# Slot scatters of two batches written together, and the search for the order of all instructions run again, in an attention and mixture-of-experts kernel

## The chip, the cores and the metric

The kernel runs on one core of one Trainium2 chip. The metric is the time of one execution on the device in microseconds (us). Before the change three runs gave a median of 989.69 us (986.74 to 997.49). A further execution was recorded by the profiler; it took 985.76 us, of which 983.7 us lie between its first and its last instruction (the span). All rows below come from that one execution.

The engines are called PE (matmul), PEld (its weight loads), DVE, ACT, POOL and SP. SP computes nothing here; it issues transfers.

## The reference

```python
def rmsnorm(x, g):
    return x / np.sqrt(np.mean(x * x, axis=-1, keepdims=True) + 1e-06) * g
q_n, k_n = rmsnorm(q, g_q), rmsnorm(k, g_k)      # q, k, v: (8, 12, 448, 64)
scores = 1.0 / np.sqrt(64) * np.matmul(q_n, k_n.transpose(0, 1, 3, 2))
attn = np.exp(scores - scores.max(-1, keepdims=True))
attn = attn / (attn.sum(-1, keepdims=True) + 1e-09)
x = np.matmul(attn, v).transpose(0, 2, 1, 3).reshape(3584, 768)

logits = x @ w_gate                               # 8 experts
e_idx = np.argmax(logits, axis=1)                 # one expert for each token
gate_w = softmax(logits)[range(3584), e_idx]
eom = 1.0 / (1.0 + np.exp(-(x @ w_output_gate)))
for e in range(8):
    mask = e_idx == e
    h = np.maximum(x[mask] @ w1[e], 0.0)          # 768 -> 1024
    out[mask] = gate_w[mask, None] * eom[mask, e, None] * (h @ w2[e])
```

## The kernel before, in words

**Two stages.** The first is attention with the routing of the tokens, the second the eight experts. The first stage works on pairs of heads: a batch has 6 pairs, so there are 48, numbered i = 0 to 47. Float32 values are split into an fp16 high part and an fp16 low part, and a product is made of three fp16 products.

**One pair.** `Lt` loads q and k (tile `qkt`). `sq`, `mh`, `ms`, `n`, `qg` normalise them. `hi` and `lo` split them into tile `X`, and SP transposes both parts into tile `ss` (`Th` for the high part, `Tl` for the low one; line L601). On PE, `M0` to `M3` multiply high parts alone to find the row maxima, which DVE reduces (`x0` to `x3`, tile `Z`). `NT` and `nt` turn the maxima around. `S0` to `S3` make the scores less the maximum (tile `pss`). `e`, `f` and `p` make the exponentials and their low parts (`p` is L685, on POOL or on DVE). `A0` to `A6` multiply with v into one PSUM bank, `bank_a`. `av1`, `av2` (tile `rc`) and `av` (tile `xr`) divide by the row sum on DVE; only then may `A0` of the next pair write the bank. `tr`, `th`, `lg`, `la` transpose the result and sum up the logits of the gate.

**Routing.** After the 6 pairs of a batch b, `r{b}.first` to `r{b}.val` pick each token's expert and its place (slot) in that expert's list. Four scatters `r{b}.z0` to `z3` on POOL (L925, `tab<-val,slot`) then write number and weight of 112 tokens each into a table in HBM. The experts later read the table to gather their tokens.

**What sets the order.** Nothing is ordered by hand. `Order.run` is a planner: it knows for each operation its engine, a duration, what it waits for, which buffer rings it holds, and a key. On each engine it takes, of the operations that are ready by its own reckoning, the one with the lowest key, and writes the instructions down in that order, which the chip then follows engine by engine. The keys come from the tables `ORDER` (four numbers for each operation of a pair) and `SHIFT` (one for each of the others). `SECOND` says, pair by pair, whether an operation that two engines can do goes to the first or the second of them. For a transfer the planner adds `lat`, the time until it has landed, and `xfer`, for how long it holds the one line in which the planner sees all transfers wait. Where the planner sees PE idle for long it writes dummy matmuls (L1473, `bank_a<-nil`) to keep PE active.

**The second stage** is written in a fixed order by `moe`, except for its beginning: the first expert's tokens (`ti0`, `xg0`, `xh0`, `xl0`, `xt0`; tiles `tie`, `xge`, `x16e`, `xTe`) and weights (`ld`, `wh`, `wl`; tiles `wste`, `w0he`, `w0le`) are planned among the last pairs, so that its first product (L1269 to L1271) can follow the last pair. The tokens of expert 0 are gathered as soon as the slots of batch 6 are in the table.

Of the kernel before, what the change touches and what calls it, by code (L numbers as in the profile page):

```python
# [52 lines left out]
    ("Lt", -1541.068, 1.677, 1123.974, -3.183),  # L53
    ("sq", 166.144, -220.427, 190.481, -54.246),
    ("mh", 159.818, -3.125, 104.389, 5.287),
    ("ms", 1654.033, 375.716, 0.250, 431.806),
    ("n", 551.031, -8.140, 172.786, 3247.925),
    ("qg", -0.547, -872.245, -2.714, 16.920),
    ("hi", 2613.749, 51.225, -727.417, 20.921),
    ("Th", 1224.882, -2107.533, -676.244, 4.206),  # L60
    ("lo", 111.461, 11.612, 1262.051, 1.977),
    ("Tl", 1.545, -2.870, 1456.809, 0.776),
    ("M0", -1345.132, -4.028, -113.895, -1.939),
    ("x0", 36.980, 9010.506, 1329.451, 1.959),
    ("M1", -2.241, 100.513, -909.486, 0.149),
    ("x1", 608.011, 17.341, -0.367, -618.082),
    ("M2", -5482.967, 14.685, 421.979, -0.160),
    ("x2", -40.558, 1.246, 95.915, -1.934),
    ("M3", -10.471, 10.436, 1.367, -0.606),
    ("x3", -0.247, 18.302, -113.316, 0.192),  # L70
    ("NT", 4.526, -2.542, -27.126, -365.406),
    ("nt", -423.381, -66.627, 436.237, 0.703),
    ("S0", 0.577, 0.094, 2069.489, -0.612),
    ("e0", -3.632, -247.548, 101.520, 1.675),
    ("f0", -749.332, -2.522, 1.532, -0.093),
    ("p0", 3.590, 1.506, 160.998, 6.230),
    ("S1", -0.528, -9.144, 303.627, 0.420),
    ("e1", -204.641, 1126.114, -0.554, -813.297),
    ("f1", 4.356, 13.958, -4.391, 8.716),
    ("p1", 126.230, -1037.208, 3.646, 1.070),  # L80
    ("S2", 0.890, -54.590, 1930.221, -0.702),
    ("e2", -2.506, 14.444, 324.586, -657.467),
    ("f2", 540.362, 925.892, -2165.612, 0.154),
    ("p2", -2.390, 395.783, 318.133, -413.006),
    ("S3", -0.173, -46.677, 156.691, -3.198),
    ("e3", -39.653, -12.452, -2.907, -0.161),
    ("f3", -42.192, 813.999, 1.848, 1.742),
    ("p3", -8954.383, -66.083, 437.056, 5.186),
    ("Lv", 307.167, -399.620, 2.028, 0.347),
    ("vh", -51.574, 13.836, 1122.447, 9.050),  # L90
    ("vl", 3.377, -27.833, 1857.127, -0.140),
    ("A0", 183.060, -8.172, 4581.120, 3.050),
    ("A1", 49.095, 358.907, -66.223, 484.461),
    ("A2", -23.494, 6.575, 147.243, -68.363),
    ("A3", 10.693, 870.234, 378.391, -1094.638),
    ("A4", 377.730, 1829.632, -509.308, 37.460),
    ("A5", 5.057, -1036.297, -1031.958, 3.872),
    ("A6", 111.289, 50.560, 10.150, 6.072),
    ("av1", -17.835, -40.302, -0.734, 0.797),
    ("av2", -3.174, -26.893, 0.998, -120.693),  # L100
    ("av", -32.125, 1.874, -447.062, 2.901),
    ("tr", -5.451, -22.518, -0.430, 8.606),
    ("th", -13.076, -28.146, 602.450, 40.981),
    ("lg", 56.165, -1284.148, 420.074, 480.839),
    ("la", 120.553, 469.327, -8.211, 2.397),
# [11 lines left out]
STICK = 22.539  # L117
# [17 lines left out]
    "p0": "011110 010010 111110",  # L135
    "p1": "101011 010001 100001",
    "p2": "110000 000000 101000",
    "p3": "111001 000101 001000",
    "lo": "111000 010001 000110",
    "vh": "001101 001000 000110",  # L140
    "th": "001100 000001 001001",
    "n": "011010 000100 110011",
    "qg": "111010 100101 001110",
    "nt": "001001 100110 001101",
    "ms": "111100 111011 110010",
    "sq": "010000 000000 110010",
# [7 lines left out]
    "k.cst": 169.441,  # L154
    "k.gd": 0.934,
    "k.wg": 5.408,
    "k.blank": -705.083,
    "k.xs": -6.407,
    "k.tab": 6.203,
    "k.g": -3.552,  # L160
    "k.ltri": 0.102,
    "k.flat": -5.412,
    "k.edges": -1.869,
    "s0": 841.221,
    "r": 4.116,
    "st": -228.929,
    "s": -344.165,
    "r-2": -1534.073,
    "r-1": -3.042,
    "open1": -814.841,  # L170
    "open2": -2.457,
    "ld0": 3.365,
    "wh0": -3.210,
    "wl0": 1.491,
    "ld1": -225.412,
    "wh1": -492.219,
    "wl1": -13.263,
    "ld2": -12.985,
    "ti0": -190.958,
    "xg0": -8.726,  # L180
    "xh0": -1155.543,
    "xl0": -1.884,
    "xt0": -3.974,
    "ti1": -228.290,
    "xg1": 4.112,
    "xh1": 5.976,
    "xl1": -0.744,
    "xt1": 73.295,
    "ti2": -492.239,
    "xg2": -469.933,  # L190
    "xh2": 199.918,
    "xl2": -12.676,
    "xt2": -5.019,
    "units": -12.564,
    "g1": -3.361,
    "hh": 589.316,
    "hl": -88.333,
    "g2": 104.405,
    "o0": -2.815,
    "o1": -2.734,  # L200
    "sc": -384.484,
    "k.id": -0.297,
    "k.sel0": 1061.513,
    "k.sel1": -218.223,
    "k.zero": -260.024,
    "w": 1.148,
    "z0": -492.602,
    "z1": -4.622,
    "z2": 6759.920,
# [1438 lines left out]
```

## Time and profile before

| | |
|---|---|
| median of three runs | 989.69 us (986.74 to 997.49) |
| profiled execution | 985.76 us, span 983.7 us, granted clock 0.987 |
| PE, PEld | 933.8 us busy (95%), 671.3 us (68%) |
| DVE, ACT, POOL | 619.5 us (63%), 554.1 us (56%), 426.0 us (43%) |
| first product of the experts (L1269) | at 521.0 us |

An engine's busy time is the union of its instructions' times. The time outside the span, 985.76 less 983.7, is 2.1 us. PE is busy in nearly all of the span, so other engines cost time only where PE waits for them, or where PE runs at the lower of its two clocks (the granted clock is then 0.50).

### The profile page before, as it was taken

How to read it: one execution, taken by the hardware profiler on the slowest of the kernel's cores; microseconds unless marked ns; L12 is line 12 of the kernel's file. 1: busy time of each engine (PE TensorE's matmuls, PEld its weight loads, DVE VectorE, ACT ScalarE, POOL GpSimd, SP SyncE). 2: the span in 40 equal slices, each digit the busy share in tenths (PEclk: the TensorE clock that was granted, in tenths of full speed). 3: DMA queues.
4: the chain of work that ended last, by engine and by line, in shares of the span. 5: the costliest groups of instructions: out<-in, count | busy, mean ns of one | idle time of the engine just before them, and what ended most of it. 6: DMA issues, size and time to landing. Idle time of an engine off the chain costs nothing. (4 is left out here: it accounts for less than half of the span.)

```text
span 983.7 us, 28910 instructions
## 1 busy us (share of the span) xinstructions
PE 933.8 (95%) x12551; PEld 671.3 (68%) x12551; DVE 619.5 (63%) x1043; ACT 554.1 (56%) x820; POOL 426.0 (43%) x325
## 2 busy tenths in 40 slices
PE   7898989999999999999989999999999999999997
PEld 3676667676777767777776686686776767665664
DVE  7879985897988888896565546428335263545310
ACT  6686876797887877868653435325234242525110
POOL 4476858678595988865532303112121111111101
PEclk9999998999999999999989999999999999999999
DMA  6848695686966968553655878839738386678101
GB/s 189 171 125 178 158 163 103 160 160 137 168 138 165 174 147 169 131 91 80 181 174 162 238 252 242 219 85 259 183 113 231 105 242 179 191 203 226 62 1 48
DMA packets 182542, 157.41 MB, mean 160 GB/s; under 512 B 152448, under 2 KB 160262, under 8 KB 176268
## 3 DMA queue, kind: packets, MB, share of 16 engines
q1 hardware_dynamic: 176652, 133.28, 56.8%
q0 software_dynamic: 5760, 22.25, 7.5%
q8 instruction: 100, 1.64, 0.7%
q14 instruction: 30, 0.25, 0.1%
HBM read 96.73 MB, written 22.59 MB: 121 GB/s over the span
## 5 line engine op out<-in xcount | busy, mean ns | idle before, releaser
L631 DVE TENSOR_REDUCE Z<-psM 128x2 f16<-128x896 f32 x168 | 178.4, 1084 | 35.2 <-PE psM L616 33.3
L685 POOL TENSOR_TENSOR pl<-p,ph 128x896 f16<-128x896 f32 x76 | 143.2, 1890 | 81.2 <-DVE psl L883 18.9
L717 PE MATMUL bank_a<-vf,pf 128*128 128x65 f32 (+1 forms) x896 | 150.7, 282 | 7.1 <-DVE xr L735 6.8
L1284 POOL DMA_INDIRECT out<-oe,tie x24 | 26.2, 1094 | 258.8 <-DVE oe L1306 222.3
L658 PE MATMUL pss<-ss 64*128 64x448 f16 (+1 forms) x1152 | 125.4, 354 | 6.7 <-ACT pf L670 3.3
L717 PEld LDWEIGHTS bank_a<-vf,pf 128*128 128x128 f32 (+1 forms) x896 | 111.0, 182 | 26.7 <-issue 10.1
L1269 PE MATMUL g1e<-xTe,w0he 128*128 128x384 f16 x384 | 125.2, 326 | 0.0
L1271 PE MATMUL g1e<-xTe,w0le 128*128 128x384 f16 x384 | 125.2, 326 | 0.0
L1270 PE MATMUL g1e<-xTe,w0he 128*128 128x384 f16 x384 | 125.2, 326 | 0.0
L721 PE MATMUL bank_a<-vh,pl 128*128 128x65 f16 (+1 forms) x1088 | 123.9, 196 | 0.2 <-POOL pl L685 0.2
L721 PE MATMUL bank_a<-vh,ph 128*128 128x65 f16 (+1 forms) x1088 | 123.6, 196 | 0.0
L719 PE MATMUL bank_a<-vl,ph 128*128 128x64 f16 (+1 forms) x1088 | 123.3, 194 | 0.0
L680 ACT ACTIVATE ph<-pss 128x896 f16<-128x896 f32 x112 | 102.3, 924 | 17.5 <-PE pss L664 17.4
L721 PEld LDWEIGHTS <-ph 128*128 128x128 f16 (+1 forms) x1088 | 111.1, 118 | 0.0
L721 PEld LDWEIGHTS <-pl 128*128 128x128 f16 (+1 forms) x1088 | 91.2, 101 | 0.3 <-POOL pl L685 0.3
L719 PEld LDWEIGHTS <-ph 128*128 128x128 f16 (+1 forms) x1088 | 91.3, 103 | 0.0
L1271 PEld LDWEIGHTS <-w0le 128*128 128x128 f16 x624 | 60.6, 98 | 24.8
L676 ACT ACTIVATE p<-pss 128x896 f32<-128x896 f32 x76 | 68.6, 915 | 15.7 <-PE pss L664 15.6
L1270 PEld LDWEIGHTS <-w0he 128*128 128x128 f16 x624 | 60.7, 98 | 23.9
L1269 PEld LDWEIGHTS <-w0he 128*128 128x128 f16 x624 | 60.7, 98 | 23.8
L597 POOL TENSOR_TENSOR X<-qkt,X 128x512 f16<-128x512 f32 x62 | 70.8, 1169 | 13.9 <-ACT X L593 6.2
L670 ACT ACTIVATE pf<-pss,lnv 128x896 f32<-128x896 f32 x56 | 56.4, 1010 | 31.2 <-PE pss L664 31.2
(328 smaller groups left out, 2284.6 us busy)
## 6 DMA issues: line engine op xcount, KB each, us to landing
wste<-w SPq DMA_DIRECT2D x48, 1024.0 KB, 7.0
qkt<-qkt SPq DMA_DIRECT2D x48, 448.0 KB, 4.6
vf<-v SPq DMA_DIRECT2D x48, 260.0 KB, 3.6
xs<-xr SPq DMA_DIRECT2D x16, 576.0 KB, 4.7
ss<-X SPq DMA_TRANSPOSE x96, 3.5
xs<-xr SPq DMA_DIRECT2D x16, 96.0 KB, 6.5
tab<-val,slot POOLq DMA_INDIRECT x32, 5.0
xge<-xs,tie POOLq DMA_INDIRECT x24, 4.9
```

The lines of the kernel that those rows point to most:

```text
L597: return [E.tensor_tensor(out=X[:, 1, :, :, d], in0=x, in1=X[:, 0, :, :, d], op=ALU.subtract) for x, d in sides(self.qkt.pop(i))]
L631: V.tensor_reduce(out=o, in_=m, op=ALU.max, axis=AX.X, negate=True)
L658: T.matmul(out, lhsT=side(wk, 1, h, 128 * u, n, x), rhs=side(wq, 0, h, 0, S, x), start=k == 0, stop=False)
L676: A.activation(out=t, in_=st[f"S{u}"], func=AF.Exp)
L680: A.activation(out=t, in_=st[f"S{u}"], func=AF.Exp)
L685: return (V if eng == DVE else Pl).tensor_tensor(out=t, in0=st[f"e{u}"], in1=at[f"ph{u}"], op=ALU.subtract)
L717: T.matmul(out, lhsT=st[f"pf{u}"][:, k, q], rhs=vf[:, jv, :], **go)
L719: T.matmul(out[:, 0:D], lhsT=at[f"ph{u}"][:, k, q], rhs=vl[:, jv, :], start=False, stop=False)
L721: T.matmul(out, lhsT=at[f"p{'hl'[w // 2]}{u}"][:, k, q], rhs=vh[:, jv, :], **go)
L1269: nc.tensor.matmul(o, lhsT=wh[:, sl], rhs=xT[:, 0, k, 0:n], start=k == 0, stop=False)
L1270: nc.tensor.matmul(o, lhsT=wh[:, sl], rhs=xT[:, 1, k, 0:n], start=False, stop=False)
L1271: q["mm"] = nc.tensor.matmul(o, lhsT=wl[:, sl], rhs=xT[:, 0, k, 0:n], start=False, stop=k == KD - 1)
```

## The change

Three things change; the arithmetic of the reference does not.

1. Scatters. Before, `z0` of a batch waits for its own slots and weights, and `z1`, `z2`, `z3` moreover for the division `av` of the second, third and fourth pair of the next batch (not in the last two batches). Now the four scatters of batches 0, 2 and 4 wait for slots and weights of the next batch too, and the waits for `av` are gone. So eight scatters come together, once in two batches. Batches 6 and 7 stay by themselves.
2. The planner's price of a scatter. Before, each holds the transfers for 350 ns; now the first of a batch 2,200 ns and the others 300. Its landing changes from 2,900 to 3,200 ns (first) and 3,000 (others); in the last two batches it was 5,500 for each and is that now for the first alone.
3. All keys (`ORDER`, `SHIFT`), the choice of engines (`SECOND`) and `STICK` have new numbers.

```diff
 ORDER = (
-    ("Lt", -1541.068, 1.677, 1123.974, -3.183),
+    ("Lt", -479.694, -2.008, -6.167, 6.015),
...
-STICK = 22.539
+STICK = 20.629
...
 SECOND = {
-    "p1": "101011 010001 100001",
+    "p1": "101010 010001 100100",
-    "n": "011010 000100 110011",
+    "n": "001010 000100 100100",
...
 SHIFT = {
-    "z0": -492.602,
-    "z1": -4.622,
-    "z2": 6759.920,
-    "z3": 48282.823,
+    "z0": -2.299,
+    "z1": -0.686,
+    "z2": 7651.187,
+    "z3": 60387.755,
...
         for c in range(NC):
-            add(f"z{c}", POOL, 1040, "slot val" + f" av.{NP * b + NP + c}" * (c > 0 and b < self.B - 2) + ("".join(f" r{b - 1}.z{k}" for k in range(NC)) if b else " k.tab k.blank"), lambda c=c: scatter(c), (), 5500 if b >= self.B - 2 else 2900, 350)
+            add(f"z{c}", POOL, 1040, "slot val" + f" r{b + 1}.slot r{b + 1}.val" * (b % 2 == 0 and b < self.B - 2) + ("".join(f" r{b - 1}.z{k}" for k in range(NC)) if b else " k.tab k.blank"), lambda c=c: scatter(c), (), (5500 if b >= self.B - 2 else 3200) if c == 0 else 3000, 2200 if c == 0 else 300)
```

PE gets the same products as before. Of the dummy matmuls L1473 there are 598 in place of 653; 272 in place of 306 stand ahead of `A0` of pair 0, and none of the 36 that stood before `M1` of pair 14 and before `M2` of pairs 21, 27 and 33 is left. Five `p` move from POOL to DVE, three `n` and one `qg` from DVE to POOL, seven `vh` from ACT to DVE.

**Three places in the order.** The first is POOL where batch 0 is scattered before: `pl9_2` is `p2` of pair 9, `X2` with `qkt14` is `lo` of pair 14, `slot0` are the slots of batch 0.

```order
L685 TENSOR_TENSOR pl9_2_2763<-p329_2_2720,ph9_2_2742 128x896
L925 DMA tab_87<-val_83,slot0_2513 30720x2 x2
L597 TENSOR_TENSOR X2_120<-qkt14_1707,X2_120 128x8x64 x2
L685 TENSOR_TENSOR pl10_1_2958<-p3210_1_2887,ph10_1_2903 128x896
L925 DMA tab_87<-val_83,slot0_2513 30720x2
L685 TENSOR_TENSOR pl10_2_3026<-p3210_2_2976,ph10_2_3010 128x896
```

The same place on POOL now, from `p2` of pair 9 to `p2` of pair 10:

```order
L685 TENSOR_TENSOR pl9_2_2751<-p329_2_2685,ph9_2_2711 128x896
L597 TENSOR_TENSOR X2_120<-qkt14_1672,X2_120 128x8x64 x2
L685 TENSOR_TENSOR pl10_1_2853<-p3210_1_2779,ph10_1_2795 128x896
L597 TENSOR_TENSOR X0_118<-qkt15_1757,X0_118 128x8x64 x2
L597 TENSOR_TENSOR X1_119<-qkt16_1882,X1_119 128x8x64 x2
L570 TENSOR_TENSOR sq21_3028<-sq21_3028 128x14x32
L685 TENSOR_TENSOR pl10_2_3064<-p3210_2_2964,ph10_2_3040 128x896
```

And POOL two batches on, where batches 0 and 1 are scattered now. Two scatters of batch 0 have gone out nine operations of other kinds earlier, just ahead of `lo` of pair 22; the other six are here, beside `p` of pairs 18 and 19:

```order
L580 TENSOR_TENSOR qkt28_4065<-qkt28_4065,y41_4401 128x896
L580 TENSOR_TENSOR qkt29_4204<-qkt29_4204,y41_4401 128x896
L585 TENSOR_TENSOR qkt29_4204<-qkt29_4204,g_75 128x448
L925 DMA tab_87<-val_83,slot0_2478 30720x2 x2
L685 TENSOR_TENSOR pl19_3_4649<-p3219_3_4533,ph19_3_4550 128x896
L685 TENSOR_TENSOR pl18_1_4685<-p3218_1_4631,ph18_1_4647 128x896
L925 DMA tab_87<-val_83,slot1_3852 30720x2 x4
```

All scatters of batch 0 have left the neighbourhood of pairs 9 and 10. Counted as runs of scatters with no other POOL work between them, those of batches 0 to 5 stand in 15 runs before (each of one or two) and in 10 now: 2, 2, 4 for batches 0 and 1; 4, 2, 2 for 2 and 3; 3, 1, 2, 2 for 4 and 5.

The second place is DVE where pair 3 is divided (`rc3`, `xr0`), before; `pl5_1` is `p1` of pair 5:

```order
L597 TENSOR_TENSOR X1_119<-qkt7_372,X1_119 128x8x64 x2
L585 TENSOR_TENSOR qkt9_904<-qkt9_904,g_75 128x448
L685 TENSOR_TENSOR pl5_1_1659<-pss5_1_1586,ph5_1_1619 128x896
L726 TENSOR_SCALAR rc3_1666<-bank_a_70 128x7
L729 RECIPROCAL rc3_1666<-rc3_1666 128x7
L735 TENSOR_TENSOR xr0_1075<-bank_a_70,rc3_1666 128x7x64
```

The same on DVE now:

```order
L597 TENSOR_TENSOR X1_119<-qkt7_367,X1_119 128x8x64 x2
L585 TENSOR_TENSOR qkt9_870<-qkt9_870,g_75 128x448
L726 TENSOR_SCALAR rc3_1631<-bank_a_70 128x7
L729 RECIPROCAL rc3_1631<-rc3_1631 128x7
L735 TENSOR_TENSOR xr0_1041<-bank_a_70,rc3_1631 128x7x64
```

`p1` of pair 5 no longer stands ahead of the division of pair 3; it has gone to POOL.

The third place is DVE where pair 45 is divided (`rc45`, `xr7`), before; `w0le0` is the low part of expert 0's weights, `x16e0` that of its tokens:

```order
L1166 SCALAR_TENSOR_TENSOR w0le0_10834<-wste0_0_10612,w0he0_10833 128x1024 x2
L726 TENSOR_SCALAR rc45_10979<-bank_a_70 128x7
L729 RECIPROCAL rc45_10979<-rc45_10979 128x7
L1166 SCALAR_TENSOR_TENSOR w0le0_10834<-wste0_1_10836,w0he0_10833 128x1024
L735 TENSOR_TENSOR xr7_10452<-bank_a_70,rc45_10979 128x7x64
L1237 TENSOR_TENSOR x16e0_0_11001<-xge0_10831,x16e0_0_11001 128x768
```

The same on DVE now:

```order
L1166 SCALAR_TENSOR_TENSOR w0le0_10647<-wste0_1_10619,w0he0_10646 128x1024 x2
L685 TENSOR_TENSOR pl46_2_10861<-pss46_2_10784,ph46_2_10838 128x896
L726 TENSOR_SCALAR rc45_10902<-bank_a_70 128x7
L729 RECIPROCAL rc45_10902<-rc45_10902 128x7
L735 TENSOR_TENSOR xr7_10352<-bank_a_70,rc45_10902 128x7x64
L1166 SCALAR_TENSOR_TENSOR w0le0_10647<-wste0_2_10799,w0he0_10646 128x1024
L1237 TENSOR_TENSOR x16e0_0_10947<-xge0_10694,x16e0_0_10947 128x768
```

The weight split has left the middle of the division. Between the last `A` of pair 45 and `A0` of pair 46, PE has `lg` of pair 43 and `S0` of pair 47 before, and `S0` of pair 46, `S2` of pair 47, `tr` of pair 44 and `S0` of pair 47 now.

## Rows read from the trace of the kernel before

**Rows 1.** The page: span, busy time and share of the engines.

```profile
span 983.7 us, 28910 instructions
...
PE 933.8 (95%) x12551; PEld 671.3 (68%) x12551; DVE 619.5 (63%) x1043; ACT 554.1 (56%) x820; POOL 426.0 (43%) x325
```

**Rows 2.** Windows: stretch, length, busy time by engine, granted clock (PEclk), DMA share, GB/s.

```profile
83.42:86.82 3.40, 3.40 (x49) 2.77 (x46) 2.42 (x4) 1.42 (x3) 3.40 (x4) 0.50 0.94 234
144.86:155.08 10.22, 10.21 (x84) 7.55 (x86) 4.40 (x7) 4.29 (x7) 5.20 (x4) 0.50 0.38 98
503.26:510.08 6.82, 6.82 (x83) 6.66 (x84) 2.88 (x4) 1.61 (x2) 0.00 (x0) 0.50 0.80 151
520.84:983.65 462.81, 455.63 (x3879) 305.80 (x3879) 202.34 (x274) 161.68 (x214) 75.47 (x65) 1.00 0.61 169
```

**Rows 3.** Waits of PE from 60 to 520.84 us: total, times, longest.

```profile
PE bank_a L717 <- DVE xr L735: 6.2, 6, 2.2
PE psM L616 <- DMA ss<-X: 4.4, 2, 3.9
```

**Rows 4.** Timeline of SP at 135.5 us (start, length): `Th` of pair 14.

```profile
135.50 2.59 SPq L601 DMA_TRANSPOSE ss<-X  x1
```

**Rows 5.** Timeline of POOL at 135 us: `z0` and `z1` of batch 0.

```profile
135.36 1.13 POOL L925 DMA_INDIRECT tab<-val,slot  x1 [0.17 <-DVE Z L631]
136.80 0.95 POOL L925 DMA_INDIRECT tab<-val,slot  x1 [0.30 <-issue]
```

**Rows 6.** Timeline of PE at 144.9 us: `M2` of pair 14; in brackets the idle time before.

```profile
144.87 0.56 PE L616 MATMUL psM<-ss 64*128 64x448 f16 x2 [3.89 <-DMA ss<-X]
```

**Rows 7.** Line L601, all 96 transposes of `X`.

```profile
DMA to landing us min/median/max: 3.0/3.5/6.0
```

**Rows 8.** Line L925, all 32 scatters.

```profile
DMA to landing us min/median/max: 2.3/5.0/8.0
```

**Rows 9.** Line L925 from 136.7 to 137.7 us, the scatter issued at 136.80 alone.

```profile
DMA to landing us min/median/max: 7.8/7.8/7.8
```

**Rows 10.** Line L925 from 475 to 481 us: the four scatters of batch 6.

```profile
L925 POOL DMA_INDIRECT tab<-val,slot x4: 938/942/943, 475.8 to 479.6; - x4
...
DMA to landing us min/median/max: 3.7/4.1/5.7
```

**Rows 11.** Timeline of PE at 82.9 us: `tr` of pair 2.

```profile
82.85 0.63 PE L745 MATMUL pstr<-cst,xr 128*128 128x128 f32 x4 [1.57 <-DVE xr L735]
```

**Rows 12.** Timeline of DVE at 80.7 us: `p1` of pair 5.

```profile
80.65 1.08 DVE L685 TENSOR_TENSOR pl<-pss,ph 128x896 f16<-128x896 f32 x1
```

**Rows 13.** Timeline of PE at 503.1 us: `A0` of pair 46.

```profile
503.14 0.62 PE L717 MATMUL bank_a<-vf,pf 128*128 128x65 f32 x2 [2.20 <-DVE xr L735]
```

**Rows 14.** Timeline of DVE at 500 us: within the division of pair 45.

```profile
499.88 2.67 DVE L1166 SCALAR_TENSOR_TENSOR w0le<-wste,w0he 128x1024 f16<-128x1024 f32 x1
502.47 0.61 DVE L735 TENSOR_TENSOR xr<-bank_a,rc 128x448 f32<-128x448 f32 x1
```

**Rows 15.** Timeline of PE from 118.1 us: `lg` of pair 5, and `A0` of pair 7.

```profile
118.14 0.42 PE L757 MATMUL pslg<-xT,wg 128*32 128x112 f32 x8
...
118.69 0.44 PE L717 MATMUL bank_a<-vf,pf 128*128 128x65 f32 x2
...
120.55 0.44 PE L717 MATMUL bank_a<-vf,pf 128*128 128x65 f32 x2 [1.15 <-DVE xr L735]
```

**Rows 16.** Groups of instructions: the dummy matmuls; busy, mean ns, idle before.

```profile
L1473 PE MATMUL bank_a<-nil 128*128 128x56 f16 x653 | 21.2, 191 | 1.2 <-DVE xr L735 1.2
```

**Rows 17.** Tile xTe at 514.9 us: the last transpose of expert 0's tokens.

```profile
L1247 SPq DMA_TRANSPOSE xTe<-x16e x1: 1448/1448/1448, 514.9 to 514.9; - x1
...
DMA to landing us min/median/max: 3.7/3.7/3.7
```

**Rows 18.** Timeline of PE at 521 us: the first product of the experts.

```profile
521.00 0.33 PE L1269 MATMUL g1e<-xTe,w0he 128*128 128x384 f16 x1
```

**Rows 19.** Timeline of SP at 289 us: `Th` of pair 29.

```profile
288.96 1.23 SPq L601 DMA_TRANSPOSE ss<-X  x1
```

**Rows 20.** Timeline of PE at 292.7 us: `M2` of pair 29.

```profile
292.68 0.69 PE L616 MATMUL psM<-ss 64*128 64x448 f16 x4
```

More of the change, by code (lines that the diff above doesn't have):

```diff
@@ L64 @@
[L64 to L85, printed above, removed]
@@ L97 @@
[L97 to L105, printed above, removed]
+    ("Lt", -479.694, -2.008, -6.167, 6.015),
+    ("sq", -4.752, -417.839, 3790.106, -0.585),
@@ new lines @@
+    ("S1", -1.051, -0.577, 1488.111, 0.068),
+    ("e1", -372.287, 33.550, -91.059, 40.625),
+    ("f1", 2.884, 65.836, 166.124, 2.197),
+    ("p1", 829.204, 3.407, 114.788, 9.633),
+    ("S2", -0.084, -48.663, 3455.910, -0.021),
+    ("e2", 2.989, 268.778, -472.353, -194.937),
+    ("f2", 252.451, 0.426, -116.588, -233.241),
+    ("p2", 2.914, 3.142, -1083.311, -176.328),
+    ("S3", 11.912, -14.950, -5.055, -21.970),
+    ("e3", -0.780, 1.029, -3.038, -2.847),
+    ("f3", -0.676, 566.316, -2.785, 2.314),
@@ new lines @@
+    ("p3", 2.810, 1311.103, 15.226, 4.011),
+    ("Lv", -1.085, 521.693, -389.705, 638.477),
+    ("vh", -97.421, 268.590, -48.130, 4.144),
+    ("vl", 0.494, -17.571, 5.327, -0.303),
+    ("A0", 253.322, 166.429, -411.335, -3.910),
+    ("A1", 17.766, 6623.530, -338.481, 351.146),
+    ("A2", -186.211, 0.473, -1.144, 0.611),
+    ("A3", -2.787, 317.529, 441.011, -349.866),
+    ("A4", 264.275, 1.470, -472.097, 6.182),
+    ("A5", 4.708, -397.767, 0.097, 4.513),
+    ("A6", 108.465, 29.428, 94.964, 3.438),
@@ L153 @@
 SHIFT = {
[L154 to L206, printed above, removed]
-    "z0": -492.602,
-    "z1": -4.622,
-    "z2": 6759.920,
-    "z3": 48282.823,
+    "k.cst": 0.540,
+    "k.gd": -9.009,
+    "k.wg": -4.035,
+    "k.blank": -4.137,
+    "k.xs": 3.492,
+    "k.tab": 0.586,
+    "k.g": -1.407,
+    "k.ltri": -4.270,
+    "k.flat": 220.207,
+    "k.edges": 154.898,
+    "s0": -1.990,
+    "r": 0.833,
+    "st": -251.004,
+    "s": -369.577,
+    "r-2": -3.945,
+    "r-1": -139.884,
+    "open1": 32.584,
+    "open2": -2.221,
+    "ld0": -1.147,
+    "wh0": -4.189,
+    "wl0": -0.646,
+    "ld1": -2.526,
+    "wh1": 32.217,
+    "wl1": -1.633,
+    "ld2": -350.188,
+    "ti0": -4.052,
+    "xg0": -2.771,
+    "xh0": -684.761,
+    "xl0": 1097.191,
+    "xt0": 7651.016,
+    "ti1": -979.915,
+    "xg1": -4.365,
+    "xh1": -3.812,
+    "xl1": 351.201,
+    "xt1": 2.555,
+    "ti2": 66439.632,
+    "xg2": 1.275,
+    "xh2": -3.256,
+    "xl2": 289.223,
+    "xt2": -0.998,
+    "units": -1.053,
+    "g1": -6.471,
+    "hh": 2.983,
+    "hl": 1.410,
+    "g2": 0.576,
+    "o0": 0.507,
+    "o1": -1236.661,
+    "sc": -0.991,
+    "k.id": -0.316,
+    "k.sel0": -1142.315,
+    "k.sel1": -0.918,
+    "k.zero": -2.612,
+    "w": -304.938,
+    "z0": -2.299,
+    "z1": -0.686,
+    "z2": 7651.187,
+    "z3": 60387.755,
 }
```

70 lines of the change are left out of this document (39 added, 31 removed).

## Prediction

> **What bounds the kernel now.** I began with the page: PE is busy 933.8 of 983.7 us, no other engine more than 63% [rows 1]. So time can only be won where PE waits or runs slowly. Windows by stretch then split the span. From 520.84 us on, the experts' stage, PE is busy 455.6 of 462.8 us at the full clock [rows 2]; its order is written down and the change leaves it alone, so I hold these 463 us fixed. The change must earn or lose its time in the first 521 us. PE's waits there are led by two kinds: the bank of the products with v is not yet free (6.2 us in 6 waits), and a transposed tile has not landed (4.4 us in 2, one of 3.9) [rows 3]. The third view is the windows of granted clock: 0.50 (1.2 of 2.4 GHz) for 3.4, 10.2 and 6.8 us [rows 2], each straight after one of PE's longer waits: 1.57 us [rows 11], 3.89 us [rows 6] and 2.20 us [rows 13]. PE is busy in all of them, so half their length is lost: 1.7, 5.1 and 3.4 us. A wait here costs more than its length.
>
> **The wait at batch 0's scatters.** `Th` of pair 14 was issued at 135.50 us [rows 4], 0.14 us after the first scatter and 1.3 before the second [rows 5]. PE got the tile at 144.87 [rows 6]: 9.4 us, where the median transpose takes 3.5 and the slowest one shown 6.0 [rows 7]. The second scatter landed 7.8 us after 136.80, at 144.6 [rows 9], 0.2 us before PE went on. So I put the delay on the scatters. The Trainium skill (page "DMA: Bandwidth & Descriptors", section "Queues, rings and completion order") says that the increment which reports a transfer done lands only after every earlier write of that transfer engine, across its queues. By that rule a transpose behind a scatter reports late even though its data have moved; the trace agrees in the 0.2 us above. The change takes batch 0's scatters away from pairs 9 and 10, and the next transposes there have only loads beside them. Gain: 3.9 of wait and 5.1 of half clock, **-9.0 us**.
>
> **What the scatters cost in their new places.** The same 24 scatters of batches 0 to 5 now stand in 10 runs, not 15. The trace has no run of eight or six; the nearest is batch 6's four, issued from 475.8 to 479.6 with a slowest landing of 5.7 [rows 10], so that the last is down by 485.3 at the latest, 9.5 us after the first issue. Batch 0's two were under way from 135.36 to 144.6, 9.3 us. A longer run exposes later transfers for no longer than a short one, so I price by the run. Before, 15 runs cost PE the two transfer waits, 4.4 us [rows 3], and the 5.1 of clock: 9.5, or 0.63 a run. Ten runs: **+6.3**. The bounds are 0 (no run meets a transpose that PE needs soon) and a full 9.0 for each group that does. POOL itself: one issue follows another by (479.6 - 475.8) / 3 = 1.27 us [rows 10], so a run of four holds POOL for 5.1 us, and `p2` of pair 18, queued behind batch 1's four, is up to 2.6 later than behind a run of two. Its readers are the `A`s of that pair, and PE has scores and maxima of later pairs in between; I take 0, with 2.6 for each such run as the bound.
>
> **The division of pair 3.** `tr` of pair 2 waited 1.57 us for DVE [rows 11], and `p1` of pair 5, 1.08 us from 80.65 on [rows 12], stood directly ahead of the division; it goes to POOL. So the wait falls by 1.1. Half clock followed for 3.4 us; PE's dummies, 38 of them, fill part of it, so I count half of its 1.7: **-1.9** in all, bounds 0 and -3.3.
>
> **The division of pair 45.** `A0` of pair 46 waited 2.20 us [rows 13], since a weight split of 2.67 us stood between reciprocal and division [rows 14]. It has left, and PE has four operations instead of two to do meanwhile. With the 3.4 us of clock, 5.6 could go. But what would be late next is the start of the experts: the last transpose of expert 0's tokens was issued at 514.9 and landed 3.7 later [rows 17], at 518.6, and the first product began at 521.00 [rows 18]. That chain begins with batch 6's slots and is not made shorter by PE, so I count only the **-2.4** between the two. Bounds 0 and -5.6.
>
> **Smaller ones.** `lg` of pair 5 moves from ahead of the last `A` of pair 6 to behind it, into the 1.15 us for which `A0` of pair 7 waited; it lasts from 118.14 to 118.69 [rows 15]: **-0.6**. Dummies: 55 fewer at 21.2 / 653 = 0.032 us [rows 16] is 1.8, but 34 of them stand in the first microseconds, where PE waits for data anyway; I take **-1.2**, bounds -0.7 and -1.8. `A0` of pair 20 now has only `NT` between it and the pair before, with four small DVE operations inside the division; that costs about one wait of the kind of [rows 3], 6.2 / 6 = 1.0. The similarly bare `A0` of pair 31 has got five PE operations ahead of it in exchange: 0. The five `p` that go to DVE, 5 x 1.08 [rows 12] = 5.4 us, and the seven `vh` are set against three `n` and one `qg` that leave it. DVE is busy (619.5 - 202.3) / 520.8 = 80% of the stage [rows 1, 2], and PE is its bound, so I take 0; if that cover goes, up to 5.4.
>
> **Sum.** -9.0 + 6.3 - 1.9 - 2.4 - 0.6 - 1.2 = -8.8 us. Against the profiled execution's own 985.76 us (span and 2.1 around it) that makes 977.0. The median of the runs shown, 989.69, is 3.9 higher, and that execution was faster than all three; I take half the distance: **979 us**. A measurement of this kernel can tell about 1%, some 9.9 us, from no change.
>
> **Rivals.**
> *The groups catch the transposes.* In the steady part `Th` is tight: for pair 29 it is issued at 288.96 [rows 19] and its tile read at 292.68 [rows 20], 3.7 us later, with a median landing of 3.5 [rows 7]. A scatter that lands after up to 8.0 us [rows 8] and holds back what is issued behind it makes PE wait up to 4.5. If each of the three groups does that once at the price of batch 0, 27 us stand in place of 6.3: 985.76 + 27 - 15.1 = 997.7, and with the 2.0 above about 1000. It decides between one hit and two: 9.0 against gains of 15.1, 18 against 15.1. The skill's rule speaks for it, because it lets a scatter delay reports that share no data with it. Against it: 14 of the 15 runs before cost PE 0.5 us of transfer waits together, though `Th` was as tight there. Chance 0.13 for three hits or more.
> *The wait moves.* The gain comes, but one new long wait with its half clock stands elsewhere, from a scatter or from one of the new neighbours on DVE, such as `A0` of pair 20. With 9.0 instead of the average 6.3, and the two divisions giving back their 4.3: 985.76 - 8.8 + 2.7 + 4.3 = 984.0, and 2.0 more is 986. For it: the planner's durations are as before, and what PE waited for in these rows is what the planner had not foreseen. Against: the two known bad neighbourhoods on DVE are gone. Chance 0.30.
> *It was not the scatters.* If `Th` of pair 14 was late from the loads ahead of it on SP's queue, the 9.0 stays and the 6.3 does not come: 985.76 - 6.1 = 979.7, or 982 with the 2.0. Against it is the 0.2 us between landing and release. Chance 0.05. A related doubt, that the scatters are not together at all, is half true in the order: 2, 2 and 4 for the first two batches, with other POOL work between. It is in the price by runs.
>
> **How the numbers follow.** Forecast 0.52, with 971 to 986 as its own range; the others 0.13, 0.30 and 0.05. No hit at all gives 979 - 6.3 = 973, and all gains at their bounds some 5 less; two hits give 979 + 11.7 = 991. The range, 968 to 996, leaves out most of three hits and little below. Faster by over 1% (below 979.8) is a little over half of the forecast's case and a share of the moved wait: 0.44. Slower by over 1% (above 999.6) is most of the first rival: 0.11. Within 1%: 0.45.
>
> **What will show it.** Right: no wait of PE for `ss` over 1 us near pair 14, the full clock there, no wait over 1 us ahead of `tr` of pair 2 and `A0` of pair 46, the first product of the experts some 9 us earlier, and an experts' stage of 463 us as before. If the wait for expert 0's tokens shows ahead of that product, the cap at pair 45 was right. Waits for `ss` beside the groups of scatters, with 0.50 in the clock behind them, would show the first rival. Wrong would be the whole way of counting if PE's waits outside these places, small ones of DVE above all, came out several microseconds larger or smaller: nothing in rows of before can show what a newly searched order does everywhere else.

## The result: 0.6% slower, and the profile after

The changed kernel takes 994.02 us (median of 20 runs, 987.65 to 999.81) where the kernel before takes 987.71 on the same chip (20 runs, 981.88 to 997.49): a ratio of 1.0062, 95% interval 1.0035 to 1.0089, about 6 us slower. Run again beside other kernels it was 1.0058 [1.0029, 1.0087]. The forecast was 979. It moved the other way, inside the range.

The page of the changed kernel, span and first engines [rows 1]:

```profile
span 994.1 us, 28776 instructions
...
PE 937.3 (94%) x12496; PEld 672.1 (68%) x12496; DVE 622.6 (63%) x1050; ACT 552.8 (56%) x812; POOL 423.4 (43%) x324
```

Its windows, to be held against [rows 2]: the stretch that ran at half clock before, four of its own five stretches at half clock, and the experts' stage.

```profile
144.86:155.08 10.22, 9.76 (x201) 7.46 (x199) 9.35 (x14) 9.77 (x15) 8.69 (x7) 1.00 0.72 125
195.97:202.80 6.83, 6.83 (x60) 5.39 (x61) 2.67 (x4) 2.94 (x5) 6.75 (x6) 0.50 0.14 53
230.10:236.93 6.83, 6.62 (x64) 5.58 (x61) 3.02 (x5) 6.54 (x10) 3.74 (x4) 0.50 0.90 208
318.85:325.68 6.83, 6.47 (x80) 4.50 (x81) 3.71 (x4) 4.60 (x6) 0.00 (x0) 0.50 0.19 22
499.76:506.58 6.82, 6.82 (x83) 6.66 (x84) 3.90 (x4) 4.73 (x6) 0.00 (x0) 0.50 0.91 314
531.20:994.10 462.90, 455.52 (x3879) 305.88 (x3879) 202.03 (x274) 162.32 (x215) 76.62 (x65) 1.00 0.61 170
```

The experts' stage is 462.9 us, as before. Its first product begins at 531.2 instead of 521.0 us, so all the loss is in the first stage (10.2 us between these two executions, about 6 between the medians). What was to go at pair 14 is gone: 1.00 stands where 0.50 stood. But half clock has come at four new places; with 3.42 us at 250.58 it is 30.7 us in all.

Waits of PE in the changed kernel from 60 to 531 us (total, times, longest), beside [rows 3]:

```profile
PE bank_a L717 <- DVE xr L735: 3.8, 6, 1.2
...
PE pss L664 <- issue: 2.8, 7, 0.8
...
PE psM L616 <- ACT ph L680: 2.6, 2, 2.4
...
PE psM L616 <- DMA ss<-X: 0.8, 2, 0.5
```

In this execution the wait for transposes has nearly vanished (4.4 to 0.8), so the first rival of the prediction, three hits of that kind, did not happen; in a second profile of the changed kernel there is one, 2.06 us at 345.93 with 6.83 us at half clock behind it. New are a wait of 2.4 us for ACT and waits that nothing in the profile explains ("issue": with PE's other lines 2.8 + 1.2 + 0.6 + 0.4 = 5.0 us, against 0.4 before). The wait for ACT comes back in the second profile (2.34). The issue waits are 3.3 us there, but 2.9 in a second profile of the kernel before, so that most of this difference was chance of one execution. The first profile's timeline shows both kinds beside scatters (first POOL's scatters, then who waits at 193, then PE at 317 us):

```profile
190.18 1.13 POOL L925 DMA_INDIRECT tab<-val,slot  x1 [0.16 <-issue]
191.62 0.95 POOL L925 DMA_INDIRECT tab<-val,slot  x1 [0.30 <-issue]
...
193.06 0.53 ACT L690 ACTIVATE vh<-vf 128x384 f16<-128x384 f32 x1 [1.86 <-PE psM L616]
...
193.06 0.17 DVE L726 TENSOR_SCALAR rc<-bank_a 128x7 f32<-128x7 f32 x1 [2.69 <-PE psM L616]
...
194.44 0.37 PE L616 MATMUL psM<-ss 64*128 64x448 f16 x2 [2.43 <-ACT ph L680]
...
317.77 0.35 PE L658 MATMUL pss<-ss 64*64 64x448 f16 x1 [0.64 <-issue]
...
319.21 0.44 PE L664 MATMUL pss<-nt,sel 64*64 64x128 f16 x8 [0.53 <-issue]
```

Two scatters of batch 0 go out at 190.18 and 191.62; ACT and DVE go on together at 193.06, half a microsecond after the second has left POOL; PE waits 2.43 us for ACT's next exponential and then runs at half clock for 6.8. At 317 us the third and fourth scatter of batch 2 go out (316.00 and 317.31), PE starves three times, and half clock follows again.

### The profile page after: what moved, and what is told of

Read it like the earlier page. It is cut to its first block, busy times and chain, and to the rows that moved or that the text cites. A ratio compares the mean times of both kernels' runs of the same rounds, so it can differ in the third digit from the quotient of the medians.

```text
span 994.1 us, 28776 instructions
## 1 busy us (share of the span) xinstructions
PE 937.3 (94%) x12496; PEld 672.1 (68%) x12496; DVE 622.6 (63%) x1050; ACT 552.8 (56%) x812; POOL 423.4 (43%) x324
## 5 line engine op out<-in xcount | busy, mean ns | idle before, releaser
L685 POOL TENSOR_TENSOR pl<-p,ph 128x896 f16<-128x896 f32 x71 | 133.8, 1890 | 112.9 <-ACT ph L680 29.4
L658 PE MATMUL pss<-ss 64*128 64x448 f16 (+1 forms) x1152 | 127.4, 356 | 13.9 <-DVE Z L631 3.8
L721 PE MATMUL bank_a<-vh,pl 128*128 128x65 f16 (+1 forms) x1088 | 126.2, 197 | 1.9 <-POOL pl L685 1.3
L721 PE MATMUL bank_a<-vh,ph 128*128 128x65 f16 (+1 forms) x1088 | 126.0, 198 | 0.8 <-issue 0.8
L719 PE MATMUL bank_a<-vl,ph 128*128 128x64 f16 (+1 forms) x1088 | 125.5, 195 | 0.0
L721 PEld LDWEIGHTS <-ph 128*128 128x128 f16 (+1 forms) x1088 | 112.6, 119 | 1.6 <-issue 1.6
L719 PEld LDWEIGHTS <-ph 128*128 128x128 f16 (+1 forms) x1088 | 92.6, 104 | 0.0
L676 ACT ACTIVATE p<-pss 128x896 f32<-128x896 f32 x71 | 64.6, 917 | 37.9 <-PE pss L664 35.0
L664 PEld LDWEIGHTS <-sel 64*128 64x128 f16 (+1 forms) x1536 | 53.5, 99 | 34.7 <-issue 7.2
```

The source lines that it names most:

```text
L658: T.matmul(out, lhsT=side(wk, 1, h, 128 * u, n, x), rhs=side(wq, 0, h, 0, S, x), start=k == 0, stop=False)
L676: A.activation(out=t, in_=st[f"S{u}"], func=AF.Exp)
L685: return (V if eng == DVE else Pl).tensor_tensor(out=t, in0=st[f"e{u}"], in1=at[f"ph{u}"], op=ALU.subtract)
L719: T.matmul(out[:, 0:D], lhsT=at[f"ph{u}"][:, k, q], rhs=vl[:, jv, :], start=False, stop=False)
L721: T.matmul(out, lhsT=at[f"p{'hl'[w // 2]}{u}"][:, k, q], rhs=vh[:, jv, :], **go)
```

## The experiments

Theory 1: the scatters cost the time, at their new places. Rival, theory 2: the newly searched order of everything else costs it. Times are ratios to the kernel before on the same chip, 1% being 9.9 us; a difference of two ratios has the root of the summed squares of their half intervals as its own. The ratio is an estimate over the executions of both kernels; the quotient of the two medians can lie up to half a percent beside it. Each edit is cut to the lines that matter. In edits `placed(order)` is the list that the planner returns, with the scatters alone put at other places in it; no other operation changes its order.

**The scatters left out, in both kernels.**

```diff
         def scatter(c):
+            if b < self.B - 2:
+                return None
```

> The changed kernel without the 24 scatters of batches 0 to 5 (these tokens' entries of the table stay blank, so the experts gather and write next to nothing; only the first stage is read here, by the start of the first expert product, 531.1 us in the changed kernel and 521.0 in the kernel before). Order of everything else as in the changed kernel. Theory 1, the scatters in their groups cost the time through other transfers than the transposes (loads of v, whose fp16 copy ACT makes late; and what PE's sequencer waits for): the waits of PE at 192, 227 to 228, 317 to 319, 340, 460 and 492 us go, with the half clock behind three of them, 8 to 13 us, so the first product begins at 518 to 523. Theory 2, the newly searched order of the other operations costs it: the scatters are worth no more than 3 us and the first product begins at 528 to 531.

> The kernel before without the 24 scatters of batches 0 to 5 (their entries of the table stay blank, only the first stage is read). The prediction priced them at 9.5 us, all of it at pair 14. By that the wait of 3.9 us before M2 of pair 14 and the half clock behind it are gone and the first product of the experts begins at 511 to 513 instead of 521.0. If the transpose there was late from the loads ahead of it on its own queue, the wait stays and the first product begins at 520 to 521.

Measured: 0.9922 [0.9885, 0.9959] for the changed order, 0.9977 [0.9949, 1.0006] for that of before. The 24 scatters cost the changed kernel 1.38% ± 0.42 (from 1.0060, the mean of its two ratios), 13.6 us, and the kernel before 0.23% ± 0.28, 2.3 us. Without them the new order is the better one by 0.55% ± 0.46, 5.4 us. Theory 2 falls, and the experts' stage, 463.8 and 463.4 us in the two profiles, is as long as before. The first product of the experts begins at 506.2 and 514.5 us, earlier than theory 1 had it (518 to 523) and later than the prediction's price had it (511 to 513). In the profile of the changed order without scatters PE has no issue wait left and two short stretches at half clock, 6.8 us in all:

```profile
44.50:506.20 461.70, 432.14 (x8121) 335.97 (x8120) 385.27 (x719) 359.45 (x545) 298.26 (x201) 0.99 0.67 149
202.32:205.73 3.41, 3.41 (x27) 1.62 (x28) 3.19 (x7) 1.86 (x6) 3.41 (x3) 0.50 0.64 147
253.52:256.93 3.41, 3.41 (x52) 2.29 (x47) 1.09 (x1) 2.56 (x4) 3.41 (x3) 0.50 0.94 198
```

The first row is a window from `A0` of pair 0 to the first expert product: PE is idle in 461.70 - 432.14 = 29.6 us of it. The same window of the changed kernel, 44.10 to 531.20, has 445.91 of 487.10 busy: 41.2 idle and 30.7 at half clock. So 11.6 us of idle and (30.7 - 6.8) / 2 = 12.0 of clock separate the two profiles, 23.6 of the 25.4 by which the windows differ. They come from two chips. The second profile of the changed kernel, from the chip of the kernel without scatters, says the same: of the 21.2 us by which its window (44.50 to 527.40) is longer, 10.0 are idle and 10.2 clock (27.3 us at half clock). Single executions differ by several us, so the ratios give the size; the windows show that waits and the clock behind them share it about evenly.

**A stand-in on POOL.** Does a scatter cost by holding POOL, or by its transfer?

```diff
+            if b < self.B - 2:
+                return nc.gpsimd.tensor_copy(out=self.scr[:SC, 0, 0:1], in_=t["slot"][:, c : c + 1]), nc.gpsimd.tensor_copy(out=self.scr[:SC, 0, 1:2], in_=t["val"][:, c, 1:2]), [nc.gpsimd.memset(self.scr[:, 1:], 0) for _ in "ab"]
```

> As the changed kernel without scatters of batches 0 to 5, but each of them is replaced on POOL by two small copies that read its slots and weights and two fills of a tile, estimated at 1.2 us together from the fill of the same tile at the start (0.49 us) and the small ones beside it, which is about the distance of two scatters of a run. POOL is so held for about as long as by the scatters, at the same places, and moves nothing. Theory 1 (transfers): the first product begins within 2 us of the kernel without scatters. Theory 3 (POOL is held, and what stands behind the runs on POOL is late): within 2 us of the changed kernel, 529 to 533.

Measured: 0.9989 [0.9956, 1.0021], first product at 511.0 us. Both expectations miss; it lies between. As far as small copies and fills hold POOL as a scatter does, holding POOL costs 0.67% ± 0.50, 6.6 us, and what is left to the transfers is 0.71% ± 0.39, 7.0 us. Both are clear of zero, but the shares are loose: in single profiles from this chip the first product begins at 506.2 us without scatters, 511.0 with the stand-ins and 527.4 in the changed kernel's second profile, which gives POOL under a quarter.

At one place the two can be told apart: `M1` of pair 18, which waited 2.43 us.

```profile
193.19 0.36 PE L616 MATMUL psM<-ss 64*128 64x448 f16 x2 [0.70 <-ACT ph L680]
```

With the stand-ins at the same place on POOL it waits 0.70 us, as without scatters (0.69). In all six profiles with two scatters there (the changed kernel's two, the three with shifted dummies and one by the rule of before, below) it waits 2.34 to 2.43, with a single one 1.06. So this wait belongs to the scatters themselves and not to POOL's time.

**Grouping in the order of before, and its stand-in.**

```diff
+        t0 = max(order.done[f"r{b + 1}.{x}"] for x in ("slot", "val")) + 300
+        for k, n in enumerate(names):
+            o, at = order.byname[n], t0 + GROUPED[b // 2][k]
+GROUPED = ((0, 1300, 24600, 25900, 32700, 34000, 35300, 36600),
+    (0, 1300, 2600, 3900, 16800, 18100, 25500, 26800), (0, 1300, 2500, 5900, 11200, 12400, 15700, 16900))
```

> The kernel before with the scatters of batches 0 to 5 taken together two batches at a time, in groups and at distances as the trace of the changed kernel shows them (2, 2, 4; then 4, 2, 2; then 3, 1, 2, 2), all else in the order of before. Theory 1a: grouping is the cost in this order too, and the time rises to 1.006 to 1.014 of before, though the wait at pair 14 goes. The prediction's price by the run: batch 0's 9.0 us go and the time falls to 0.990 to 0.997. Theory 2b, only the changed kernel's order is sensitive at the places of its groups: 0.996 to 1.002.

> The kernel before with its scatters gathered as in the changed kernel, but each replaced on POOL by the same small copies and fills as in the stand-in of the changed kernel (the table stays blank for these tokens). If the 8.3 us that gathering costs there are POOL's, 1.005 to 1.011 of before; if they are the transfers', 0.996 to 1.002.

Measured: 1.0084 [1.0053, 1.0115], as expected if grouping is the cost, and 1.0036 [1.0004, 1.0068] with the stand-in, between its two expectations. In the order of before, too, the groups are dear: 0.84% more than at the places of before, though batch 0's scatters are gone from pairs 9 and 10. Against the kernel without scatters, POOL's hold is 0.59% ± 0.43 and the transfers 0.48% ± 0.45. In the stand-in's timeline one of PE's waits has POOL behind it, though no scatter moves anything: eight fills and copies (342.21 to 344.69) stand on POOL ahead of a `sq` for which DVE, idle for 4.92 us, waits, and PE for DVE (`sq` could have begun up to 2.4 us earlier, at the end of POOL's `p` at 342.26):

```profile
348.61 0.56 PE L616 MATMUL psM<-ss 64*128 64x448 f16 x2 [5.26 <-DVE pl L685]
```

**One by one, and by the rule of before.** If grouping is the cost, taking the groups apart should help.

```diff
+            o, at = order.byname[n], max(t0 + (4500 if b == 4 else 9000) * k, order.start[n] if k == 0 else 0)
```

```diff
+            at = max([at + 1300] + [order.done[x] + 300 for x in [f"r{b}.slot", f"r{b}.val"] + [f"av.{NP * b + NP + c}"] * (c > 0)])
```

The first line puts them one by one, the second by the rule of before, in batches 0, 2 and 4 or in all six; the first try at that lacked the `at + 1300`.

> The changed kernel once more, beside the next three on one chip: 1.003 to 1.009 times the time of before, as measured first, and in its profile the waits of PE that nothing in the profile explains (issue) come back beside runs of scatters, some 5 us in the first stage, against under 1 us in the kernels without scatters.

> The changed kernel with the same 24 scatters of batches 0 to 5 one by one, from the place of the first on, 9 us of the planner's time apart (4.5 in batches 4 and 5), all else in its order. Theory 1a, a run of scatters that are under way together is what holds the other transfers: the time falls by 6 to 11 us from the changed kernel, to 0.995 to 1.000 of before, and PE's issue waits are gone. Theory 1b, each scatter costs about the same wherever it stands (13.8 us between the changed kernel and the one without scatters, 0.6 a scatter): within 3 us of the changed kernel.

> The changed kernel with the scatters of batches 0, 2 and 4 at the places that the rule of before gives them (z0 with its own slots, z1 to z3 behind a division of the next batch each), all other operations in the order of the changed kernel, and the scatters of batches 1, 3 and 5 where they are. Nothing is left out. Theory 1: the waits behind the groups shrink, 4 to 8 us, while batch 0's scatters return to pairs 9 and 10 and can cost up to 9 there: first product between 522 and 534, with waits for transposed tiles or for ACT near 140 us. Theory 2: within 2 us of the changed kernel, and the waits of PE between 180 and 240 us are the same as there.

> The changed kernel with the scatters of batches 0, 2 and 4 by the rule of before (the first with its own slots, the others behind a division of the next batch each, 1.3 us of the planner's time apart at least), the rest in its own order. In the first kernel of this kind two scatters stood in reverse order, and one waited about 5 us on POOL for the landing of the other at two places, which made its time; here they don't. Runs of four are left only for batch 1. If runs of four and the groups cost what the changed kernel loses, 0.993 to 0.999 of before; if the scatters cost alike wherever they stand in this order, 1.002 to 1.008.

> The same with batches 1, 3 and 5 by that rule too, so that all 24 scatters stand as before would put them, in the order of the changed kernel. If each order loses by its scatters what before loses (2.3 us), 0.992 to 0.998 of before: a kernel faster than both. If this order suffers from them anywhere, 1.002 to 1.010.

Measured: the changed kernel again 1.0058; one by one 1.0031 [1.0003, 1.0058]; batches 0, 2 and 4 by the old rule 1.0159 [1.0110, 1.0209] at the first try and 1.0040 [1.0018, 1.0062] without its flaw; all six batches by it 1.0130 [1.0102, 1.0159]. The first try tells nothing on groups: in it the second scatter of the list waited on POOL, 4.78 us at 268.66 for another's landing and 5.40 at 137.92, where the profile names a load. The others say that the loss needs no run of four. Singles gain 0.27% ± 0.40 of 1.38, so at most about half. And the rule whose places cost 2.3 us in one order costs 2.08% ± 0.47 in the other, more than any expectation had it. The timeline of the kernel with all six by the rule shows one way (POOL, then DVE's `vl` at 329 us, then PE):

```profile
326.04 0.94 POOL L925 DMA_INDIRECT tab<-val,slot  x1 [0.15 <-issue]
327.00 4.48 POOL L597 TENSOR_TENSOR X<-qkt,X 128x512 f16<-128x512 f32 x4
331.45 3.70 POOL L685 TENSOR_TENSOR pl<-p,ph 128x896 f16<-128x896 f32 x2
...
329.31 6.26 DVE L696 SCALAR_TENSOR_TENSOR vl<-vf,vh 128x384 f16<-128x384 f32 x1 [4.66 <-POOL X L597]
...
336.63 0.93 PE L658 MATMUL pss<-ss 64*128 64x448 f16 x4 [6.99 <-DVE Z L631]
```

A scatter ahead of `lo` puts it and `p` beside `vl`, which waits 4.66 us for POOL and then lasts 6.26 (all `vl` of this kernel from 60 to 320 us last 0.42 to 0.56): it ends at 335.57, 0.42 us after POOL's two `p`. `vl` reads nothing of `X`; its wait is one that the program writes in (`behind`) where the planner sees such operations of DVE and POOL close together, and the planner did not know of the moved scatter. PE waits 6.99. The Trainium skill (page "SBUF — State Buffer", section "Who interferes with whom") says that a DVE instruction with two SBUF inputs, as `vl` has, contends with one of POOL that reads SBUF; these rows agree, with 6.26 us in place of 0.56.

**A shift of PE's instructions.** Are the issue waits, and with them the rest, late packets of PE's own instructions?

```diff
+    o = max(out, key=lambda o: max(o.get("pad", 0), o.get("still", 0)))
+    o[side] += 64        # or 128, or -64
```

> The changed kernel with 64 more dummy matmuls ahead of pair 0's products, so that PE's stream of instructions, which it gets in packets of 16 KB, one in about 7 us, is shifted by 128 instructions against everything else; at 0.03 us each they cost up to 1.8 us at the start. Theory F, a packet of PE's own instructions that falls into a run of scatters comes late: the waits beside the scatters change their places; those of 2.4 us before M1 of pair 18 (192 us), 1.3 at 228 and the issue waits at 228 and 318 us fall under 0.8 each, others may come elsewhere, and the time is 3 to 10 us below that of the changed kernel (0.996 to 1.003 of before). Theory G, scatters hold something that does not depend on the place in PE's stream: the same waits stand at the same operations within 0.4 us, and the time is 1.005 to 1.011 of before.

> The same with 128 more, a shift by 256 instructions, an estimated whole packet (16 KB in 7 us against 16,200 matmuls and weight loads in 487 us). They cost up to 3.5 us at the start. Theory F: the shift by a whole packet brings the waits of the changed kernel back at the same operations (2.4 us before M1 of pair 18, issue waits beside the third run), 1.005 to 1.013 of before. Theory G: the same waits too, so that only the run with 64 tells the two apart; waits that differ here as well would speak for neither a packet of 256 instructions nor G.

> The same with 64 fewer. Theory F: the same place in the packets as with 64 more, so waits at the same operations as there, and a time 2 to 4 us below that run. Theory G: the waits of the changed kernel, 1.002 to 1.007 of before. Fewer dummies may leave PE at half clock for longer at the start, up to 3 us, which the granted clock before 60 us would show.

> The kernel before with 64 more dummies at its longest row of them. Theory F: its scatters, which cost 2.3 us at their present places in the packets, meet other packets; the waits at pair 14 (3.9 us in the first profile) and beside the other 14 runs change, and the time moves by anything from -2 to +10 us besides the 1.8 of the dummies. Theory G: 1.000 to 1.003 of before, waits as before.

Measured: 1.0085 [1.0054, 1.0115], 1.0091 [1.0057, 1.0125], 1.0098 [1.0067, 1.0129], and 1.0043 [1.0003, 1.0082] for the order of before. The time does not follow the shift (with 64 fewer it is above its expectation of 1.002 to 1.007), and the largest wait stands in all three at the same operation, 2.38, 2.39 and 2.39 us; with 64 more:

```profile
196.19 0.37 PE L616 MATMUL psM<-ss 64*128 64x448 f16 x2 [2.38 <-ACT ph L680]
```

So for that wait and the time theory F is out. One place behaves as it says: beside the first run of four of batch 2, PE's issue waits are 1.5 us with 128 more, as in the changed kernel, and 0.7 and 0.5 us with 64 more and fewer, where a wait for `ss` (1.4 and 0.9) stands instead. That is too little to settle where issue waits come from.

**The kernel before once more.**

> The kernel before once more, for a second profile. If the wait of 3.9 us before M2 of pair 14 with its half clock, on which the prediction put 9.0 us, belongs to this kernel, it stands there again, 3 to 5 us. If it was chance of one execution, the wait is under 1.5 us there and the clock stays full from about 35 to 340 us, as in the profile with 64 more dummies.

Measured: 983.62 us, and at pair 14 this timeline and these windows of the second profile:

```profile
139.29 0.36 PE L616 MATMUL psM<-ss 64*128 64x448 f16 x2 [0.43 <-DMA ss<-X]
```

```profile
82.00:86.00 4.00, 3.93 (x83) 2.97 (x79) 3.97 (x5) 2.56 (x5) 4.00 (x4) 1.00 0.92 222
137.00:155.00 18.00, 17.26 (x315) 13.61 (x307) 12.73 (x22) 17.89 (x29) 16.42 (x13) 1.00 0.99 185
```

The wait of 3.89 us [rows 6] is 0.43 here, and the clock is full; with 64 more dummies it was 1.13, at full clock too. The 9.0 us were one execution's; and without them this execution is only 2.1 us shorter than the first profile's.

**Each half of the change alone.** The edit is the last pair of lines of the diff ahead of the prediction, put into the kernel before or taken back in the changed one.

> The kernel before, all its tables, with only the new line for the scatters (what they wait for and what they cost the planner); the planner then places the scatters in runs of 4, 2, 2, then 2, 2, 2, 2, then eight, and shifts other operations a little. Theory 1a: 1.004 to 1.014 of before, most waits beside the runs. Price by the run: 0.990 to 0.998.

> All tables of the changed kernel with the line for the scatters of before, the other half of the change alone; the planner shifts operations a little. If keys and line belong together, as in the opposite case (1.031), 1.010 to 1.035 of before. If the new keys are better in themselves (0.55% without scatters) and only the grouping harms, 0.990 to 1.000.

Measured: the new line with the old keys 1.0313 [1.0278, 1.0348], the new keys with the old line 1.0273 [1.0223, 1.0323]. The first is above both of its expectations, the second where keys and line were expected to belong together. Neither half can be judged alone, since the planner then orders the rest by keys that were searched for another line; it writes 1034 and 859 dummies where the two kernels have 653 and 598.

**Scatters where POOL waits anyway.** In the profile without scatters POOL waits often and long (waits from 160 to 480 us):

```profile
POOL pl L685 <- ACT ph L680: 30.6, 8, 8.4
POOL pl L685 <- PE bank_a L721: 16.4, 4, 10.1
POOL pl L685 <- DVE rc L726: 9.4, 3, 3.8
```

```diff
+            out.remove(o)
+            out.insert(out.index(order.byname[x]), o)
+AHEAD = ("p1.14 p2.14 p2.14 p2.15", "p3.19 p3.19 p2.18 p2.20", "p2.22 p2.22 lo.30 p2.24",
+    "p2.27 p2.27 p3.31 p2.31", "p2.33 p3.37 p3.37 p2.36", "p1.40 p1.40 p3.45 p3.45")
```

> The changed kernel with its 24 scatters of batches 0 to 5 placed by hand, one or two at a time, ahead of those operations of POOL that waited longest for other engines in the profile without scatters (2 to 10 us each), all else in its order; nothing is left out. POOL's time is then free for them. If half of the 13.8 us that the scatters cost this kernel is POOL's (stand-in: 6.6), and the rest the transfers', 0.997 to 1.002 of before; if the transfers cost less in ones and twos, 0.992 to 0.997, faster than both kernels; if places chosen after the search are dear in themselves, as in the kernel by the rule of before, 1.004 and more.

Measured: 0.9876 [0.9831, 0.9920], 971.33 us (969.70 to 973.25, 6 runs) where the kernel before took 981.78 beside it. It is faster than both and below every range expected, with all work done, and 0.46% ± 0.58 below the kernel without scatters: at these places the 24 scatters cost nothing that can be measured. Its window from `A0` of pair 0 to the experts, and PE's waits:

```profile
44.00:506.10 462.10, 431.12 (x8121) 336.73 (x8120) 384.90 (x719) 358.84 (x545) 323.33 (x225) 0.99 0.72 152
```

```profile
PE psM L616 <- DMA ss<-X: 4.7, 5, 1.4
```

PE is idle for 31.0 us, there is no issue wait, and `M1` of pair 18 waits 0.57 us instead of 2.43. Transposes are waited for more than in the changed kernel, 4.7 us against 0.8 and 2.1 in its two profiles, and it is the fastest all the same. POOL's timeline shows how POOL's time is free here (the second and third scatter of batch 0):

```profile
174.05 0.95 POOL L925 DMA_INDIRECT tab<-val,slot  x1 [0.15 <-issue]
175.31 0.94 POOL L925 DMA_INDIRECT tab<-val,slot  x1 [0.30 <-issue]
178.43 1.88 POOL L685 TENSOR_TENSOR pl<-p,ph 128x896 f16<-128x896 f32 x1 [2.17 <-DVE mx L884]
```

The `p` behind them would have waited 4.5 us for DVE; it still waits 2.17.

## Why the prediction was wrong

The step that failed is **what the scatters cost**, in both places where the prediction put a number on it.

*The gain of 9.0 us at batch 0's scatters* was read from one execution. The wait, the tile, the scatter's landing and the half clock stand in that profile as they were told; the 9.4 us of the transpose run to PE's start, and its own landing is in no view (the slowest in [rows 7] is 6.0). But the second profile has 0.43 us and full clock there, and by the times all 24 scatters of the kernel before were worth 2.3 us, not 9.5. There was next to nothing to gain by moving them.

*The 6.3 us in their new places*, 0.63 for each of 10 runs, are 13.6. The price by the run rested on the same 9.5, and on the thought that a scatter hurts through a transpose behind it. In the changed kernel waits for transposes are 0.8 and 2.1 us in two profiles. What came instead: about half, with wide bounds, by POOL, which the prediction took at 0 with 2.6 us as a bound for a run; the stand-ins put it at 6.6 us here and 5.8 for groups in the order of before. The rest came with the transfers, by waits beside the scatters: surely those of ACT and DVE at 193 us and of PE behind them, which the stand-in does not have, and perhaps PE's issue waits. The Trainium skill (page "DMA: Bandwidth & Descriptors", section "Queues, rings and completion order") speaks of reports held behind earlier writes; by that the transposes would be late, and the rows here show them waited for less in the slow kernel (0.8 and 2.1) than in the fastest (4.7), so that the rule, true or not, does not explain this loss.

*The order's own terms* held in sum and not one by one. -1.9 - 2.4 - 0.6 - 1.2 = -6.1; without scatters in either kernel the new order is 5.4 us better (± 4.6). That the two sums agree is luck, since the parts do not. At pair 3 `tr` of pair 2 still waits, 1.24 us for 1.57 [rows 11], so that the move of `p1` gave 0.3 of the 1.1 us of its wait. `A0` of pair 7 still waits 1.20, so the 0.6 there did not come; `A0` of pair 20 waits 0.95, for the 1.0 set against it. At pair 45 the 2.20 us [rows 13] are gone, and the cap set on that by the experts' tokens was not there: the first product did not wait for them. The start gave more: `A0` of pair 0 begins at 44.1 us in the changed kernel, at 48.7 and 47.2 in two profiles of before. The cover over DVE's five more `p` held: without scatters PE waits about 17 us for DVE in the new order and 21 in that of before, one profile each.

So in place of -9.0 + 6.3 - 6.1 = -8.8 stand -2.3 + 13.6 - 5.4 = +5.9, which is the measured 6 by the way the three are worked out. The range held the result only because it was wide enough for the rivals. The nearest rival was the one that says that the wait moves; it had the mechanism, one new wait beside a scatter with its half clock behind, at a third of the count.

What is shown: that the scatters carry the loss (left out, it is gone), that POOL's time is a part of it, about half with wide bounds (stand-ins), that their places decide (18 us between two kernels that differ in the places of 24 scatters alone). Not settled is how the rest arises: one of its waits is found (`M1` of pair 18), with a report of PE that is late beside two scatters, and what holds that report is open. In the fastest kernel the scatters stand in ones and twos and where POOL waits; runs of four where POOL waits were not tried, so the two conditions are not told apart, though singles at other places gained only 0.27%.

## What to carry to other kernels

A stall of a few microseconds in one profile is no price until a second execution shows it, or a kernel without its supposed cause loses it. An operation that computes nothing and is waited for by nobody still holds its engine: find in the profile where that engine waits for others and put it there, by moving it alone in the finished order (0.9876 here). At other places the same kind of move lost (1.0130 by the rule of before), and so did changing the planner's line or its keys alone (1.0313 and 1.0273). Two stand-ins (left out, and replaced by work of equal length) split a cost between an engine and the transfers in two runs; how sharply depends on the spread of the executions, which here leaves the shares loose.

## What the runs showed of the hardware that was not expected

- A wait is not always followed by half clock, and the same kernel differs in that from one execution to the next. `tr` of pair 2 waits 1.57 us in both profiles of before; behind it the granted clock was 0.50 for 3.4 us in the first [rows 2, 11] and 1.00 in the second (82 to 86 us, above). Behind `M1` of pair 18 and its 2.4 us stands half clock in the changed kernel, and full clock with 64 dummies fewer.
- A report of PE can come late beside two scatters. In the changed kernel the last product of `A` of pair 14 begins at 190.76 and lasts 0.19, yet DVE's division and ACT's `vh`, which both wait for it, begin at 193.06, 2.1 us after its end; in the fastest kernel that product begins at 192.01, and the division at 192.24, 0.04 us after its end. The second profile of the changed kernel has it again (2.0 us). With the stand-ins in place of the scatters `M1` of pair 18, which waits in this chain, has 0.70 us in place of 2.43. The profile names a later product, `M` from 191.64 to 192.00, as the releaser; from its end it is still 1.1 us. What holds it was not found.
- A DVE operation beside POOL's can stretch: `vl` from 0.5 to 6.26 us in the rows above, and to 3.32 at 436.82 in the kernel with single scatters, where PE then waited 2.13 us.
